# Four block normalisations of the first layer moved from VectorE to GpSimd in a four-layer attention and MLP kernel

## The chip, the cores and the metric

The kernel runs on one core of one Trainium2 chip. A core has TensorE (PE in the profile; PEld is its weight load), VectorE (DVE), ScalarE (ACT), GpSimd (POOL), SyncE (SP, which here only issues DMAs) and 16 DMA engines. The metric is the device time of one execution in microseconds; lower is better. Inputs and outputs lie in device memory (HBM).

## What is computed

A sequence of 2048 tokens with 448 features goes through four residual layers: attention A, gated MLP B, then A and B again with the same weights. Each layer starts with a layer norm without gain or bias. Attention is local and dilated: 16 heads of 28 features, and each query sees the 8 keys at distances 0, 2, ..., 14. The MLP multiplies two linear maps elementwise, without a nonlinearity.

```python
def _layernorm(x, axis=-1, eps=1e-5):
    m = jnp.mean(x, axis=axis, keepdims=True)
    v = jnp.var(x, axis=axis, keepdims=True)
    return (x - m) / jnp.sqrt(v + eps)
...
        pos = jnp.arange(S)
        off = jnp.arange(W) * dil
        idx = pos[:, None] - off[None, :]
        mask = idx >= 0
...
        logits = jnp.einsum("bhsd,bhswd->bhsw", q, kg) * scale
        logits = jnp.where(mask[None, None, :, :], logits, -1e9)
        attn = _softmax(logits, axis=-1)
        o = jnp.einsum("bhsw,bhswd->bhsd", attn, vg)
...
        g = jnp.einsum("bsd,df->bsf", x, w_gate)
        u = jnp.einsum("bsd,df->bsf", x, w_up)
        h = g * u
        return jnp.einsum("bsf,fd->bsd", h, w_down)
...
    x = A_x
    x = x + _A_ref(_layernorm(x, axis=-1), A_wqkv, A_wo)
    x = x + _B_ref(_layernorm(x, axis=-1), B_w_gate, B_w_up, B_w_down)
    x = x + _A_ref(_layernorm(x, axis=-1), A_wqkv, A_wo)
    x = x + _B_ref(_layernorm(x, axis=-1), B_w_gate, B_w_up, B_w_down)
    return x
```

## The kernel before

**Blocks and chunks.** The tokens are split by parity, so that a dilation of two becomes a plain neighbourhood: block B (0 to 15) is 128 tokens on 128 partitions, kept in `x_sb` in bf16. Layers are numbered 0 to 3 (attention 0 and 2, MLP 1 and 3). Each layer is cut into chunks of 256 or 512 tokens; in layer 0 chunk 0 is blocks 0 and 1, then 2 to 5, 6 to 9, 10 to 13, and 14 with 15.

**The norm of a block** (`ln_chunk`) has four steps. VectorE takes statistics (`bn_stats` at L630, `bn_aggr` at L632 into `mv`). ScalarE makes 1/sqrt(variance + eps) as a logarithm and an exponential (L633, L635, into `rstd`). One `tensor_scalar` (L651) subtracts the mean and multiplies by `rstd`, both per partition, and writes `xn_sb`, a ring of five slots; in layers 0 and 2 it is 512 elements wide, in layers 1 and 3 it is 896. Last, the block is transposed into `xnTa` or `xnTb`: by a DMA transpose from SyncE (L654), or, for the first four chunks of layer 0, by eight TensorE transposes (L661) whose result in PSUM ScalarE or VectorE copies out (L669).

**Attention of a chunk.** `qk_chunk` multiplies `xnTa` with the query-key weight `WQK` (L369, four units of 14 matmuls, each cut in two parts of 6 and 8) and copies the result to `qk` (L785). `WQK` is laid out in the kernel: L565 copies the staged weight (GpSimd, eight copies of 448 elements a partition; the same line's ScalarE form is two instructions, L566 and L567), and L575 fills the four unused columns of each head with a part of the value weight (eight small copies), which may only be done when TensorE has ended the first two chunks. `v_group` makes values (`v_sb`, L851, L856). The first three query blocks use small score matmuls (L915). The later ones use `attn_front2`: four key blocks (L970, or L969 on ScalarE) are made by multiplying `qk` by a 0/1 column `pm`, 256 or 512 elements wide, and TensorE multiplies them with the queries (L977); ScalarE takes exponentials (L922, L983), VectorE multiplies by a 0/1 band (L932 with `MK`, L992 with `MB`). `attn_back` multiplies with the values (L1010), adds the two halves and normalises (L1020, L1024, L1034 to L1055), and `y_blocks` projects and adds to `x_sb` (L1073). GpSimd builds the bands `MK` and `MB` at the start (selects L523 and sums L527, L547, L548).

**MLP of a chunk.** `b_chunk`: gate and up (L369 and L372 with `WGU`), a copy (L1109), the product (L1112), down (L369 with `WD`, or L1124 for the last two blocks), the addition (L1073, L1128).

**Order.** The program lists 1636 operations, each with the engines that may do it. What each engine does, and in which order, stands in a table of strings, `ORD`; a letter behind `!` picks which of several waits comes first, `+` and `@` mix the small matmuls of attention between those of the MLP. `BANK` gives the PSUM banks of each operation. Every engine runs its list in order and waits on semaphores, so an operation that is late holds all behind it on its engine. DMAs are issued by SyncE in the order of its list, apart from three by ScalarE.

Of the kernel before, what the change touches and what calls it, by code (L numbers as in the profile page):

```python
# [404 lines left out]
def build(nc, A_x, A_wqkv, A_wo, B_w_gate, B_w_up, B_w_down, out):  # L405
# [214 lines left out]
    def ln_chunk(li, j, prio):  # L620
# [17 lines left out]
        for B in blocks:  # L638
# [12 lines left out]
            sc.add("dve", one(lambda E, B=B, dst=dst, src=src: E.tensor_scalar(dst, src, mv[:, B, 0:1], rstd[:, B:B + 1], ALU.subtract, ALU.mult), ("xn", li, B)),  # L651
                   325.0 if par == 0 else 540.0, deps=[("rstd", li, B), ("mv", li, B), ("x", li - 1, B), prev], prio=prio - 0.2)
# [602 lines left out]
```

## Time and profile before

| | |
|---|---|
| runs | 380.07, 380.54, 381.71 us (median 380.54) |
| the profiled execution's own time | 379.54 us |
| its span, first to last instruction | 377.8 us |
| mean granted TensorE clock | 0.999 |
| TensorE before 10 us | busy 8.43 of 10.00 us (start-up, with warming matmuls) |
| GpSimd, longest idle stretches | 49.8, 37.0 and 35.8 us, all before L970 in the third layer |
| L651 on VectorE, 512 wide | 32 of them, 12.8 us |
| L970 on GpSimd, all shapes | 54 of them, 82.8 us |

The page's lines give the engine, source line, operation, `out<-in`, count, busy time and mean duration, and what ended the idle time before. VectorE is busy 73% over the whole span, but 9.75 of the ten microseconds from 10 to 20; the average hides that.

### The profile page before, as it was taken

The page shows a single profiled execution, that of the slowest core. Times are in us where ns is not written, and L with a number is a line of the kernel's source. Part 1 is how long each engine was busy: PE and PEld are TensorE (multiplying, and loading weights), DVE is VectorE, ACT ScalarE, POOL GpSimd, SP SyncE. Part 2 cuts the span into 40 slices and gives each one's busy share as a digit, 9 for nine tenths or more (in the row PEclk, how much of TensorE's full clock was granted, in tenths as well). Part 3 has the DMA queues.
Part 4 walks back from the last instruction along what each step waited for, and adds up shares of the span by engine and source line. Part 5 has one row for each costly group of instructions (what it writes and reads, how often), then busy time and mean ns, then how long its engine had stood idle before and what let it go on. Part 6 is the DMA issues. An engine that isn't in the chain of part 4 may idle for free.

```text
span 377.8 us, 13091 instructions
## 1 busy us (share of the span) xinstructions
PE 372.8 (99%) x5796; PEld 220.7 (58%) x5796; DVE 277.2 (73%) x571; ACT 203.9 (54%) x382; POOL 100.3 (27%) x123
## 2 busy tenths in 40 slices
PE   8999999999999999999999999999999999999997
PEld 4556587645556885545566577554455444455764
DVE  6999999797996874788876785758758884244433
ACT  3999996857328542464634554584686333124310
POOL 8735598710000610009300076003900000000000
PEclk9999999999999999999999999999999999999999
DMA  8883638201420162104142036200520025040002
GB/s 267 208 171 86 147 69 164 57 3 29 85 57 2 33 84 40 30 2 69 21 64 30 2 46 88 53 2 12 82 55 3 1 51 122 0 62 2 2 2 97
DMA packets 55099, 22.67 MB, mean 60 GB/s; under 512 B 46132, under 2 KB 54148, under 8 KB 55044
## 3 DMA queue, kind: packets, MB, share of 16 engines
q1 hardware_dynamic: 54612, 21.34, 28.7%
q8 instruction: 45, 0.74, 0.8%
q10 hardware_dynamic: 432, 0.52, 0.4%
q14 instruction: 10, 0.08, 0.1%
HBM read 8.54 MB, written 2.71 MB: 30 GB/s over the span
## 4 chain that ended last, share of the span: by engine, by line
PE 90%; DMA 3%; DVE 3%; SPq 2%; ACT 1%; POOL 0%; issue 0%
PE ps L369 83%; PE ps L1010 2%; PE ps L977 2%; PE ps L1124 1%; PE ps L372 1%; DMA x_sb<-in_A_x_dram 1%; DMA v_sb<-vt 1%; SPq L794 1%; SPq L805 1%; DVE st L630 1%; DMA vt<-qk 1%; ACT E_sb L983 1%; POOL WQK L575 0%; SPq L468 0%; DVE xn_sb L651 0%; PE ps L661 0%
## 5 line engine op out<-in xcount | busy, mean ns | idle before, releaser
L369 PE MATMUL ps<-xnTb,WGU 64*128 64x512 bf16 (+1 forms) x1928 | 177.4, 333 | 0.0
L369 PEld LDWEIGHTS ps<-xnTb,WGU 64*128 64x128 bf16 x1928 | 99.5, 94 | 63.4 <-ACT g_sb L1109 0.3
L1109 ACT ACTIVATE g_sb<-ps 128x512 bf16<-128x512 f32 (+1 forms) x140 | 69.2, 510 | 104.8 <-PE ps L369 96.0
L970 POOL TENSOR_SCALAR qk<-qk,pm 128x512 bf16<-128x512 bf16 (+1 forms) x51 | 77.9, 1544 | 159.2 <-DVE qk L785 64.5
L1112 DVE TENSOR_TENSOR hT<-g_sb,ps 128x512 bf16<-128x512 bf16 (+1 forms) x140 | 77.3, 573 | 54.6 <-ACT g_sb L1109 52.7
L369 PE MATMUL ps<-WD,hT 64*128 64x448 bf16 x828 | 85.9, 349 | 0.0
L369 PEld LDWEIGHTS ps<-WD,hT 64*128 64x128 bf16 x828 | 40.0, 94 | 34.5 <-ACT g_sb L1109 0.2
L369 PE MATMUL ps<-xnTa,WQK 64*128 64x512 bf16 (+1 forms) x504 | 54.0, 353 | 0.3 <-POOL WQK L565 0.2
L1073 DVE TENSOR_TENSOR x_sb<-x_sb,ps 128x448 bf16<-128x448 bf16 x62 | 36.5, 614 | 17.4 <-PE ps L369 17.0
L630 DVE BATCH_NORM_STATS2 st<-x_sb 128x6 f32<-128x448 bf16 x64 | 38.1, 614 | 2.1 <-DMA x_sb<-in_A_x_dram 1.8
L651 DVE TENSOR_SCALAR xn_sb<-x_sb,mv,rstd 128x896 bf16<-128x896 bf16 (+1 forms) x64 | 35.8, 574 | 3.8 <-ACT rstd L635 3.5
L983 ACT ACTIVATE E_sb<-ps 128x1024 bf16<-128x1024 f32 (+1 forms) x32 | 31.7, 996 | 9.6 <-PE ps L977 9.6
L369 PEld LDWEIGHTS ps<-xnTa,WQK 64*128 64x128 bf16 x504 | 25.1, 94 | 18.8 <-POOL WQK L565 0.4
L369 PE MATMUL ps<-wo_g,oT 64*128 64x448 bf16 x256 | 29.8, 349 | 0.0
L785 ACT ACTIVATE qk<-ps 128x1024 bf16<-128x1024 f32 (+1 forms) x27 | 25.0, 941 | 5.8 <-PE ps L369 5.7
L369 PE MATMUL ps<-WV,xnTa 64*128 64x336 bf16 (+3 forms) x252 | 22.8, 304 | 0.0
L1035 ACT ACTIVATE R_sb<-R_sb 128x960 f32<-128x960 f32 (+1 forms) x18 | 17.3, 959 | 8.1 <-DVE R_sb L1034 8.1
L992 DVE TENSOR_TENSOR E_sb<-E_sb,MB 128x1024 bf16<-128x1024 bf16 (+2 forms) x34 | 21.2, 634 | 0.4 <-ACT E_sb L983 0.3
L633 ACT ACTIVATE lnv<-mv,eps_sb 128x2 f32<-128x2 f32 (+1 forms) x33 | 9.4, 291 | 22.4 <-DVE mv L632 22.3
L1034 DVE STREAM_SHUFFLE R_sb<-O_sb 128x960 f32<-128x960 f32 (+1 forms) x18 | 21.1, 1181 | 0.0
L1055 DVE TENSOR_TENSOR oT<-O_sb,R_sb 128x960 bf16<-128x960 f32 (+1 forms) x16 | 17.6, 1104 | 4.5 <-ACT R_sb L1036 4.5
L369 PEld LDWEIGHTS ps<-wo_g,oT 64*128 64x128 bf16 x256 | 13.5, 94 | 10.1 <-issue 0.2
(67 smaller groups left out, 239.4 us busy)
## 6 DMA issues: line engine op xcount, KB each, us to landing
out_dram<-x_sb SPq DMA_DIRECT2D x15, 112.0 KB, 1.8
WGU<-in_B_w_gate_dram SPq DMA_DIRECT2D x7, 224.0 KB, 4.3
WGU<-in_B_w_up_dram SPq DMA_DIRECT2D x7, 224.0 KB, 3.8
x_sb<-in_A_x_dram SPq DMA_DIRECT2D x3, 448.0 KB, 6.3
WD<-in_B_w_down_dram SPq DMA_DIRECT2D x2, 448.0 KB, 3.9
vt<-qk SPq DMA_DIRECT2D x42, 16.0 KB
WD<-in_B_w_down_dram SPq DMA_DIRECT2D x2, 336.0 KB, 4.2
xnTb<-xn_sb SPq DMA_TRANSPOSE x32, 3.1
```

The lines of the kernel that those rows point to most:

```text
L369: return lambda E: E.matmul(out(), lhs(), rhs(), start=start, stop=stop)
L630: sc.add("dve", one(lambda E, B=B: E.bn_stats(st6[:, B, :], x_sb[:, B, :]), ("bn", li, B)), 525.0, deps=[("x", li - 1, B)] + ([("xn", li - ...
L651: sc.add("dve", one(lambda E, B=B, dst=dst, src=src: E.tensor_scalar(dst, src, mv[:, B, 0:1], rstd[:, B:B + 1], ALU.subtract, ALU.mult), ( ...
L785: return E.activation(dst, src, ACT.Copy) if hasattr(E, "activation") else E.tensor_copy(dst, src)
L970: return E.tensor_scalar(dst, src, pm[:, t:t + 1], None, ALU.mult)
L983: return E.activation(E_sb[:, slot, 2 * c:2 * c + 2, 0:w], ps[:, bk[0]:bk[0] + 2, 0:w], ACT.Exp, scale=SCALE)
L992: return E.tensor_tensor(e, e, m, ALU.mult)
L1034: sc.add("dve", one(lambda E: E.stream_shuffle(R_sb[:, rs, 0:w], O_sb[:, op, 0:w], [DH] * 32), ("Rs", li, g)), dve_est(w) + 100.0, deps=[( ...
L1055: return E.tensor_tensor(oT[:, :, t:t + n].rearrange("p h (d n) -> p h d n", d=nd), O, R, ALU.mult)
L1073: sc.add("dve", one(lambda E: E.tensor_tensor(x_sb[:, B, :], x_sb[:, B, :], ps[:, bk[w], 0:D], ALU.add), ("x", li, B)), dve_est(D), deps=[ ...
L1109: sc.add("act", one(lambda E, gs=gs, bk=bk: E.activation(g_sb[:, gs, 0:nt], ps[:, bk[0], 0:nt], ACT.Copy), ("G", li, j, fc)), act_est(nt), ...
L1112: sc.add("dve", one(lambda E, gs=gs, bk=bk, fc=fc: E.tensor_tensor(hT[:, fc, hs, 0:nt], g_sb[:, gs, 0:nt], ps[:, bk[1], 0:nt], ALU.mult), ...
```

## The change

In `ln_chunk`, the L651 norm of layer 0 may now be done by GpSimd for blocks 4 to 15. The table then gives it blocks 8, 9, 11 and 14. All of `ORD` and `BANK` is replaced: every engine's list has the same operations for the most part, with neighbours exchanged all through the program. TensorE's matmuls are the same in number and shape. Besides the four norms, these change engines: in layer 0, the copies of three transposed blocks (7, 9, 11) go from ScalarE to VectorE, one L565 copy from GpSimd to ScalarE, two L575 copies from GpSimd to VectorE, two key blocks from VectorE to GpSimd and two the other way; in layer 2, 26 key blocks leave GpSimd (15 to VectorE, 11 to ScalarE), and 3 go from ScalarE to VectorE. Of the copies out of PSUM, 12 go from ScalarE to VectorE and 15 the other way. GpSimd's list shrinks from 119 instructions to 92.

**GpSimd between its masks and its first key blocks.** `MK`, `MB` and `hT` with L523 are mask work, `WQK` is the small weight copies, L970 the key blocks. Before:

```order
L547 TENSOR_TENSOR MB<-hT 128x72 [waits sem_pool]
L523 AFFINE_SELECT hT<-hT 128x72
L527 TENSOR_TENSOR MK<-hT 128x72 [waits sem_pool]
L575 COPY WQK<-hT 128x16x4 [waits sem_pe,sem_d_stv]
L575 COPY WQK<-hT 128x16x4 x3
L575 COPY WQK<-hT 128x4x3x4 x4
L970 TENSOR_SCALAR hT<-qk,pm 128x4x2x64 [waits sem_dve]
```

Now:

```order
L547 TENSOR_TENSOR MB<-hT 128x72 [waits sem_pool]
L651 TENSOR_SCALAR xn_sb<-x_sb,mv,rstd 128x512 [waits sem_act]
L547 TENSOR_TENSOR MB<-hT 128x72
L523 AFFINE_SELECT hT<-hT 128x72
L651 TENSOR_SCALAR xn_sb<-x_sb,mv,rstd 128x512
L651 TENSOR_SCALAR xn_sb<-x_sb,mv,rstd 128x512 [waits sem_pe,sem_act]
L575 COPY WQK<-hT 128x4x3x4 [waits sem_pe,sem_d_stv]
L575 COPY WQK<-hT 128x4x3x4 x2
L548 AFFINE_SELECT MB<-MB 128x72
L575 COPY WQK<-hT 128x16x4
L575 COPY WQK<-hT 128x4x3x4
L523 AFFINE_SELECT hT<-hT 128x72
```

and right behind it:

```order
L575 COPY WQK<-hT 128x16x4
L527 TENSOR_TENSOR MK<-hT 128x72
L651 TENSOR_SCALAR xn_sb<-x_sb,mv,rstd 128x512 [waits sem_pe]
L523 AFFINE_SELECT hT<-hT 128x72
L970 TENSOR_SCALAR hT<-qk,pm 128x4x2x64 [waits sem_act]
```

The norms of blocks 9, 8 and 14 now stand ahead of the small weight copies, that of block 11 behind them; two of the eight copies are gone to VectorE, and two selects stand among the six that are left.

**TensorE around the first steps that need the whole of `WQK`.** L661 transposes a block, L915 are scores, L1010 is the product with the values. Before:

```order
L661 MATMUL ps<-hT,xn_sb 128x64 [waits sem_act]
L661 MATMUL ps<-hT,xn_sb 128x64 x7
L1010 MATMUL ps<-E_sb,v_sb 32x72 [waits sem_dve]
L1010 MATMUL ps<-E_sb,v_sb 32x72 x31
L915 MATMUL ps<-qk 64x64 [waits sem_act,sem_dve]
L915 MATMUL ps<-qk 64x64 x63
L369 MATMUL ps<-xnTa,WQK 128x512 [waits sem_act,sem_pool]
L369 MATMUL ps<-xnTa,WQK 128x512 x5
L369 MATMUL ps<-xnTa,WQK 128x512 [waits sem_dve]
L369 MATMUL ps<-xnTa,WQK 128x512 x5
L661 MATMUL ps<-hT,xn_sb 128x64 [waits sem_act]
```

Now:

```order
L1010 MATMUL ps<-E_sb,v_sb 32x72 x31
L661 MATMUL ps<-hT,xn_sb 128x64 [waits sem_dve]
L661 MATMUL ps<-hT,xn_sb 128x64 x7
L915 MATMUL ps<-qk 64x64 [waits sem_act,sem_dve]
L915 MATMUL ps<-qk 64x64 x63
L369 MATMUL ps<-xnTa,WQK 128x512 [waits sem_dve,sem_pool]
L369 MATMUL ps<-xnTa,WQK 128x512 x5
L369 MATMUL ps<-xnTa,WQK 128x512 [waits sem_dve]
L369 MATMUL ps<-xnTa,WQK 128x512 x5
L369 MATMUL ps<-xnTa,WQK 128x512 [waits sem_pe]
L369 MATMUL ps<-xnTa,WQK 128x512 x7
L661 MATMUL ps<-hT,xn_sb 128x64 [waits sem_pool,sem_act]
```

The transpose of block 7 moved from ahead of the product with the values (L1010) to behind it, directly ahead of the scores. The last row is block 11's transpose: it now waits for GpSimd, and one more part of eight matmuls stands ahead of it.

**GpSimd's key blocks of the third layer**, L970 towards the end of its list. Before:

```order
L970 TENSOR_SCALAR qk<-qk,pm 128x4x64 [waits sem_act]
L970 TENSOR_SCALAR qk<-qk,pm 128x4x64
L970 TENSOR_SCALAR qk<-qk,pm 128x4x2x64 x3
L970 TENSOR_SCALAR qk<-qk,pm 128x4x64
L970 TENSOR_SCALAR qk<-qk,pm 128x4x2x64 [waits sem_act,sem_dve]
L970 TENSOR_SCALAR qk<-qk,pm 128x4x2x64 x2
L970 TENSOR_SCALAR qk<-qk,pm 128x4x2x64 [waits sem_pe]
L970 TENSOR_SCALAR qk<-qk,pm 128x4x2x64 x4
```

Now:

```order
L970 TENSOR_SCALAR qk<-qk,pm 128x4x2x64 [waits sem_pe]
L970 TENSOR_SCALAR qk<-qk,pm 128x4x2x64
L970 TENSOR_SCALAR qk<-qk,pm 128x4x2x64 [waits sem_dve,sem_act]
L970 TENSOR_SCALAR qk<-qk,pm 128x4x2x64 [waits sem_act]
L970 TENSOR_SCALAR qk<-qk,pm 128x4x2x64
L1204 UNCONDITIONAL_BRANCH
```

Three key blocks are left on GpSimd in that layer, of 29; the first piece shows the first 14 of them, the second the last two key blocks of the first layer and the three that are left.

The diff, with the tables cut to GpSimd's list:

```diff
 ORD = {
...
-    "pool": "18 43 20 19 23 24 25 26 27 28 29 90 91 94 95 92 96 93 97 49 53 50 22 67 60 34 38 51 35 31 64 54 39 65 40 68 21 32 66 30 69 61 62 57 55 41 58 59 33 70 63 52 56 36 37 100 102 98 104 105 103 101 99 299 71 42 300 409 426 431 432 427 553 554 581 559 558 576 628 634 633 580 575 651 650 629 656 655 801 796 820 819 814 797 961 967 989 1175 984 983 988 1174 1202 1201 1354 1179 1197 1353 1180 1196 1381 1375 1380 1376 1398 1402 1403",
+    "pool": "18 43 20 19 23 24 25 26 27 28 29 90 91 94 95 92 96 93 30 21 31 34 49 50 53 60 35 67 57 32 38 58 54 64 22 61 51 62 68 39 55 65 69 33 52 59 63 190 56 36 187 223 103 101 105 71 104 99 66 98 37 208 40 299 41 70 295 294 427 409 426 42 431 432 554 576 581 559 558 633 628 580 634 575 629 651 650 655 656 819 1197 1196",
...
 }
...
@@ -648,8 +648,8 @@
                 c0 = 512 * (nbs[(li, j)] % 2) + 128 * B - t0
                 war = xslot_users.get(nbs[(li, j)] % 2, [])
             nt = 4 if par == 0 else 7
-            sc.add("dve", one(lambda E, B=B, dst=dst, src=src: E.tensor_scalar(dst, src, mv[:, B, 0:1], rstd[:, B:B + 1], ALU.subtract, ALU.mult), ("xn", li, B)),
-                   325.0 if par == 0 else 540.0, deps=[("rstd", li, B), ("mv", li, B), ("x", li - 1, B), prev], prio=prio - 0.2)
+            sc.add(("dve", "pool") if li == 0 and B > 3 else "dve", one(lambda E, B=B, dst=dst, src=src: E.tensor_scalar(dst, src, mv[:, B, 0:1], rstd[:, B:B + 1], ALU.subtract, ALU.mult), ("xn", li, B)),
+                   {"dve": 325.0, "pool": 1620.0} if li == 0 and B > 3 else 325.0 if par == 0 else 540.0, deps=[("rstd", li, B), ("mv", li, B), ("x", li - 1, B), prev], prio=prio - 0.2)
             if not by_pe:
```

More of the change, by code (lines that the diff above doesn't have):

```diff
@@ L60 @@
 ORD = {
[5 rows of a table removed]
[5 rows of a table added]
 }
-BANK = "72:1 138:23 142:45 158:67 161:67 164:67 167:45 182:23 185:45 188:01 191:01 206:01 209:01 212:01 215:01 227:67 229:01 231:23 233:45 239:01 243:4501 248:23 256:45 258:67 260:67 262:23 268:23 272:01 277:0167 282:45 290:23 296:67 301:45 304:23 312:45 326:62 329:01 332:23 335:67 338:41 341:01 344:06 347:57 350:50 353:74 356:21 359:67 362:34 365:10 368:54 374:67 376:45 378:23 380:23 393:67 398:23 406:01 411:67 414:01 422:23 428:23 433:01 436:23 444:23 468:72 471:67 474:34 477:54 480:17 483:10 486:46 489:05 492:14 495:50 498:76 501:71 504:64 507:50 510:75 516:23 522:67 524:45 526:01 528:45 541:67 547:01 555:45 560:23 563:45 571:65 577:67 582:23 585:23 593:10 597:01 599:67 601:45 603:23 616:67 622:23 630:23 635:01 638:45 646:23 652:23 657:45 660:67 668:67 692:01 695:51 698:40 701:45 704:36 707:01 710:72 713:60 716:23 719:07 722:14 725:56 728:27 731:14 734:32 740:20 766:45 768:01 770:67 772:01 785:45 790:23 798:23 803:23 806:01 816:67 821:45 824:67 832:72 856:16 859:45 862:45 865:13 868:01 871:63 874:60 877:45 880:27 883:24 886:17 889:17 892:60 895:60 898:27 904:07 930:67 932:23 934:45 936:01 949:23 955:45 963:01 968:01 971:45 979:26 985:23 990:23 993:45 1001:10 1015:41 1018:31 1021:60 1024:23 1027:64 1030:64 1033:36 1036:51 1039:23 1042:45 1045:10 1048:01 1051:01 1054:06 1057:03 1073:67 1076:72 1079:23 1082:67 1085:14 1088:56 1091:25 1094:14 1097:03 1100:54 1103:21 1106:52 1109:43 1112:10 1115:45 1143:67 1145:45 1147:23 1149:23 1162:67 1168:45 1176:45 1181:67 1184:01 1192:67 1198:67 1203:67 1206:67 1214:01 1238:03 1241:56 1244:45 1247:72 1250:76 1253:13 1256:14 1259:10 1262:23 1265:67 1268:05 1271:52 1274:35 1277:42 1280:46 1288:01 1316:67 1318:23 1320:45 1322:45 1335:01 1341:23 1347:45 1355:67 1360:67 1363:67 1371:64 1377:01 1382:67 1385:67 1393:15 1399:23 1404:23 1407:01 1415:27 1439:52 1442:45 1445:03 1448:37 1451:46 1454:40 1457:57 1460:34 1463:16 1466:52 1469:52 1472:63 1475:17 1478:04 1481:01 1489:63 1517:45 1520:27 1523:54 1526:27 1529:63 1532:57 1535:54 1538:24 1541:45 1544:63 1547:47 1550:27 1553:47 1556:52 1559:71 1567:23 1585:61 1588:10 1591:71 1594:63 1597:50 1600:10 1603:10 1606:50 1609:54 1612:61 1615:24 1618:02 1621:53 1624:46 1627:6 1630:7 1633:0"
@@ new lines @@
+BANK = "72:2 138:01 142:45 158:45 161:23 164:23 167:01 182:45 185:67 188:45 191:45 206:67 209:01 212:01 215:67 227:01 229:67 231:23 233:01 239:67 243:2367 248:23 256:23 258:01 260:01 262:67 268:45 272:67 277:4501 282:01 290:23 296:45 301:01 304:45 312:01 326:24 329:67 332:45 335:23 338:17 341:67 344:62 347:30 350:36 353:01 356:03 359:52 362:54 365:32 368:54 374:45 376:67 378:23 380:23 393:45 398:45 406:67 411:23 414:67 422:74 428:45 433:67 436:01 444:67 468:01 471:01 474:75 477:45 480:23 483:42 486:15 489:40 492:40 495:67 498:35 501:14 504:05 507:67 510:61 516:05 522:23 524:01 526:67 528:01 541:23 547:23 555:01 560:45 563:01 571:46 577:67 582:01 585:67 593:74 597:45 599:67 601:01 603:23 616:67 622:23 630:67 635:23 638:67 646:67 652:23 657:01 660:23 668:45 692:14 695:34 698:12 701:76 704:12 707:23 710:50 713:72 716:04 719:45 722:71 725:07 728:06 731:15 734:63 740:76 766:23 768:45 770:67 772:01 785:23 790:01 798:23 803:01 806:45 816:01 821:01 824:01 832:56 856:53 859:24 862:45 865:23 868:01 871:70 874:23 877:41 880:65 883:67 886:54 889:12 892:60 895:30 898:24 904:04 930:45 932:23 934:45 936:01 949:67 955:23 963:23 968:23 971:67 979:31 985:45 990:23 993:01 1001:54 1015:67 1018:61 1021:53 1024:25 1027:63 1030:17 1033:53 1036:23 1039:65 1042:45 1045:20 1048:70 1051:45 1054:35 1057:10 1073:61 1076:04 1079:42 1082:23 1085:42 1088:26 1091:75 1094:34 1097:31 1100:34 1103:25 1106:02 1109:41 1112:53 1115:54 1143:23 1145:67 1147:23 1149:67 1162:67 1168:01 1176:67 1181:67 1184:23 1192:01 1198:67 1203:67 1206:67 1214:23 1238:21 1241:56 1244:45 1247:70 1250:10 1253:21 1256:04 1259:32 1262:13 1265:67 1268:34 1271:50 1274:14 1277:50 1280:04 1288:23 1316:01 1318:23 1320:45 1322:45 1335:67 1341:67 1347:45 1355:67 1360:67 1363:67 1371:40 1377:23 1382:67 1385:45 1393:23 1399:67 1404:01 1407:23 1415:56 1439:15 1442:01 1445:61 1448:67 1451:70 1454:41 1457:37 1460:26 1463:05 1466:70 1469:25 1472:43 1475:67 1478:14 1481:30 1489:12 1517:46 1520:47 1523:67 1526:65 1529:71 1532:07 1535:56 1538:53 1541:67 1544:04 1547:50 1550:25 1553:56 1556:32 1559:64 1567:70 1585:13 1588:04 1591:54 1594:41 1597:24 1600:32 1603:35 1606:63 1609:64 1612:15 1615:10 1618:23 1621:75 1624:21 1627:1 1630:0 1633:7"
```

8 rows, old and new, of the table ORD are left out of this document.

## The prediction

> **What bounds the kernel now.** The page comes first: its busy shares, and its chain that ended last.
>
> ```profile
> PE 372.8 (99%) x5796; PEld 220.7 (58%) x5796; DVE 277.2 (73%) x571; ACT 203.9 (54%) x382; POOL 100.3 (27%) x123
> PE 90%; DMA 3%; DVE 3%; SPq 2%; ACT 1%; POOL 0%; issue 0%
> ```
>
> TensorE is busy 372.8 of 377.8 us and holds 90% of the chain; GpSimd (POOL) holds none of it. Where TensorE has any room is told by the view of busy time by stretches (stretch, length, busy us of PE, PEld, DVE, ACT, POOL, then granted clock and DMA).
>
> ```profile
> 9.00:16.00 7.00, 6.92 (x142) 4.13 (x138) 6.75 (x23) 6.43 (x19) 6.78 (x33) 1.00 1.07 272
> 16.00:20.00 4.00, 4.00 (x55) 1.93 (x52) 4.00 (x13) 3.77 (x11) 0.72 (x3) 1.00 0.40 107
> 20.00:23.00 3.00, 2.50 (x130) 1.63 (x128) 2.99 (x10) 2.98 (x6) 1.70 (x8) 1.00 0.86 200
> 23.00:100.00 77.00, 76.82 (x1462) 47.68 (x1458) 70.93 (x146) 61.41 (x105) 37.73 (x25) 1.00 0.41 85
> 100.00:280.00 180.00, 180.00 (x2792) 109.72 (x2790) 135.67 (x274) 93.92 (x177) 45.44 (x31) 1.00 0.26 42
> ```
>
> From 9 to 280 us TensorE idles 0.08 + 0.50 + 0.18 = 0.76 us, most of it between 20 and 23, where VectorE (2.99 of 3.00) and ScalarE (2.98) are full. So hardly anything can be won after the start-up, and the question is what the change makes TensorE wait for. TensorE's timeline shows when it wants the blocks that move:
>
> ```profile
> 16.70 0.28 PE L661 MATMUL ps<-hT,xn_sb 64*128 64x64 bf16 x8
> 16.82 2.54 PE L369 MATMUL ps<-xnTa,WQK 64*128 64x512 bf16 x22
> 19.19 0.28 PE L661 MATMUL ps<-hT,xn_sb 64*128 64x64 bf16 x8
> 19.31 1.03 PE L369 MATMUL ps<-xnTa,WQK 64*128 64x512 bf16 x8
> 20.17 0.62 PE L661 MATMUL ps<-hT,xn_sb 64*128 64x64 bf16 x24
> 22.42 1.47 PE L369 MATMUL ps<-xnTa,WQK 64*128 64x512 bf16 x12
> 23.73 0.28 PE L661 MATMUL ps<-hT,xn_sb 64*128 64x64 bf16 x8
> ...
> 28.02 3.88 PE L369 MATMUL ps<-xnTa,WQK 64*128 64x256 bf16 x62
> ```
>
> L661 transposes a normalised block, eight matmuls each: block 9 at 16.70, block 8 at 19.19, block 11 at 23.73. The L369 at 22.42 is the first query-key step that needs all of the weight WQK, including the pieces that GpSimd copies (L575). Block 14 goes by a DMA transpose and is wanted only by the step at 28.02.
>
> **The change part by part.** GpSimd's own rows, before:
>
> ```profile
> 3.98 4.31 POOL L565 COPY WQK<-hT 128x448 bf16<-128x448 bf16 x8
> 8.23 0.46 POOL L508 MEMSET hT<- 128x432 bf16 x1
> 16.48 0.32 POOL L527 TENSOR_TENSOR MK<-hT 128x72 bf16<-128x72 bf16 x1
> 20.51 0.24 POOL L575 COPY WQK<-hT 128x64 bf16<-128x64 bf16 x1 [3.70 <-PE ps L661]
> 20.90 1.46 POOL L575 COPY WQK<-hT 128x64 bf16<-128x64 bf16 x7 [0.16 <-issue]
> ```
>
> GpSimd ends its masks at 16.80, idles 3.70 us until TensorE releases the weight pieces at 20.51, and ends those at 22.36, just before the step at 22.42. Into that gap go the norms. What a norm costs on GpSimd no row shows. The nearest are its key blocks (L970: same width and types, one multiplication by a per-partition scalar; the norm has a subtraction and a multiplication, with two scalars). The second row below is GpSimd between 48 and 65 us, without a gap and beside a full VectorE:
>
> ```profile
> L970 POOL TENSOR_SCALAR hT<-qk,pm x3: 1558/1570/1679, 26.5 to 34.5; 128x512 bf16<-128x512 bf16 x3
> L970 POOL TENSOR_SCALAR qk<-qk,pm 128x512 bf16<-128x512 bf16 x11 | 17.8, 1632 | 4.6 <-PE ps L977 4.6
> L970 POOL TENSOR_SCALAR qk<-qk,pm 128x256 bf16<-128x256 bf16 x7 | 6.7, 963 | 49.8 <-ACT qk L785 49.8
> L565 POOL COPY WQK<-hT 128x448 bf16<-128x448 bf16 x8 | 4.3, 574 | 0.1
> L523 POOL TENSOR_SCALAR_AFFINE_SELECT hT<-hT 128x72 bf16<-128x72 bf16 x34 | 7.6, 256 | 0.5
> L547 POOL TENSOR_TENSOR MB<-hT 128x72 bf16<-128x72 bf16 x3 | 0.9, 318 | 0.1
> L651 DVE TENSOR_SCALAR xn_sb<-x_sb,mv,rstd 128x512 bf16<-128x512 bf16 x32 | 12.8, 417 | 0.9 <-ACT rstd L635 0.6
> L970 DVE TENSOR_SCALAR hT<-qk,pm 128x512 bf16<-128x512 bf16 x3 | 1.2, 408 | 0.0
> ```
>
> Lower end: a norm costs what a key block costs, 1.57 us alone, 1.63 loaded. Upper end: the second operation doubles the work per element. From 963 to 1632 ns over 256 elements is 2.61 ns per element and 0.29 us fixed, so 0.29 + 512 x 5.22 ns = 2.96 us. Between them: a copy with the same fixed part takes (574 - 290) / 448 = 0.63 ns per element, so one operation adds 1.98; a second one adding as much gives 0.29 + 512 x 4.59 ns = 2.64 us. I take 1.63, because it is the same engine, operation and shape, and because on VectorE the two forms cost nearly the same (417 and 408 ns). That is a choice, and the range keeps both ends.
>
> The Trainium skill (GPSIMD Engine Reference, 3.1) gives 512 elements 769 ns at best and holds bodies of up to two operations to the same port limit. This trace's 1570 ns for one operation is twice that; by the skill's page a second operation is free, and the sum would be the one below.
>
> Now the queue. One weight copy goes to ScalarE: GpSimd's seven end at 3.98 + 4.31 x 7/8 = 7.75. Of the 8.57 us from 8.23 to 16.80, three mask sums (318) and four selects (256), 1.98 us, move behind the first norm. So norm 9 starts at 7.75 + 8.57 - 1.98 = 14.34 and ends at 15.97, 0.73 before it is wanted. Its scale factor is there by then:
>
> ```profile
> 14.07 0.19 ACT L635 ACTIVATE rstd<-lnv 128x2 f32<-128x2 f32 x1
> ```
>
> A sum and a select later (0.57), norm 8 runs from 16.54 to 18.17, 1.0 early; norm 14 ends at 19.80. The weight pieces wait for TensorE until 20.51 anyway: 0.71 us of cover for three norms, 0.24 each. Behind them stand six pieces and two selects instead of eight pieces:
>
> ```profile
> L575 POOL COPY WQK<-hT 128x48 bf16<-128x48 bf16 x4 | 0.9, 274 | 0.0
> L575 POOL COPY WQK<-hT 128x64 bf16<-128x64 bf16 x4 | 0.8, 236 | 3.9 <-PE ps L661 3.7 <-issue 0.2
> ```
>
> 4 x 0.274 + 2 x 0.236 + 2 x 0.256 = 2.08 against 4 x 0.274 + 4 x 0.236 = 2.04: the step at 22.42 comes some 0.1 later. Then one mask sum, and norm 11 from 22.75 to 24.38. The changed order puts one eight-matmul step (19.31 to 20.17, 0.86 us) ahead of block 11's transpose, which is thus wanted at 23.73 + 0.1 + 0.86 = 24.69: 0.3 of cover. With d the price of a norm above 1.63, TensorE loses 0.1 + max(0, 3d - 0.71) + max(0, d - 0.3) us.
>
> VectorE loses four norms (4 x 0.417 = 1.67 us) and gains three transposed copies from ScalarE and two weight pieces:
>
> ```profile
> L669 DVE COPY xnTa<-ps 128x512 bf16<-128x512 bf16 x7 | 2.8, 418 | 0.3 <-PE ps L661 0.2
> L669 ACT ACTIVATE xnTa<-ps 128x512 bf16<-128x512 bf16 x5 | 3.0, 596 | 0.5 <-PE ps L661 0.5
> ```
>
> 3 x 0.418 is 1.25; with two pieces of at most 0.24 that is 1.7, so VectorE keeps its load and ScalarE sheds 3 x 0.596. The waits of 20 to 23 could shrink, by 0.5 at most, or grow by as much, as block 7's transpose and its copy now stand right ahead of the scores (L915). I take nothing.
>
> In the third layer 26 key-block copies leave GpSimd for VectorE (15) and ScalarE (11), and three more go from ScalarE to VectorE. On VectorE one takes 0.61 (below), so 18 x 0.61 = 11.0 us in a stretch of 180 where it has 44.3 idle; ScalarE's net 8 x 0.72 = 5.8 stands against 86.1 idle. I take nothing; if a copy came late at a step, each slip would cost about one copy, 0.6 to 0.7.
>
> ```profile
> L970 DVE TENSOR_SCALAR qk<-qk,pm 128x512 bf16<-128x512 bf16 x3 | 1.8, 610 | 0.0
> L969 ACT ACTIVATE qk<-qk,pm 128x512 bf16<-128x512 bf16 x3 | 2.1, 714 | 0.8 <-DVE qk L785 0.8
> 375.54 0.35 ACTq L468 DMA_DIRECT2D out_dram<-x_sb x1
> ```
>
> SyncE issues the last outputs in another order, but the end is ScalarE's store at 375.54, behind the last matmul: nothing. The sum: span 377.8 + 0.1 = 377.9, with 1.74 around it (379.54 - 377.8) 379.6 for such an execution. The median of the runs is 1.0 above the profiled one, so 380.6; I say 380.8, since of the open terms more can lose than win.
>
> **The rivals.** *The norm's second operation is dear* (the other side). Place: GpSimd's queue ahead of the weight pieces. At 2.64 us d is 1.01: 0.1 + 2.32 + 0.71 = 3.1 us, 383.7; at 2.96, 0.1 + 3.28 + 1.03 = 4.4, 385.0. It decides from 1.87 on and passes 0.5% at 2.33 (4 x 0.70 - 1.01 + 0.1 = 1.9). For it: copy to one operation multiplies GpSimd's cost per element by four. Against: VectorE's two rows.
>
> *VectorE is held by a norm.* Its mask products (L932, two inputs from SBUF) now run beside norm 8. If each waited for the norm's end, up to 1.63 us, with VectorE full, TensorE would lose about 1.5: 382.3. Against it: L992, the same product, takes 672 ns beside a busy GpSimd and 678 without.
>
> ```profile
> L992 DVE TENSOR_TENSOR E_sb<-E_sb,MB 128x1024 bf16<-128x1024 bf16 x3 | 2.0, 672 | 0.0
> L992 DVE TENSOR_TENSOR E_sb<-E_sb,MB 128x1024 bf16<-128x1024 bf16 x5 | 3.3, 678 | 0.0
> ```
>
> The Trainium skill (SBUF — State Buffer, Who interferes with whom) says that the second to issue fully blocks. By it this rival holds; these rows disagree.
>
> *A late key block in the third layer*: two slips, +1.4, 382.1.
>
> *VectorE's relief counts*: the 0.5 of 20 to 23 goes, 380.1. With TensorE full elsewhere, no more is there.
>
> **How the numbers follow.** Chances: forecast 0.44, dear norm 0.40, held VectorE 0.05, late key blocks 0.06, relief 0.05. What a measurement can tell from no change is about 0.5%, 1.9 us. The dear norm is over that in nine of ten of its part (0.36), the two others in most (0.07), the forecast in a little (0.01): slower 0.44. Faster would need more idle time than TensorE has: 0.03. Within 0.5%: 0.53. The forecast's own range is 380.0 to 381.8; with the dear norm most of the way it is 379.9 to 384.6.
>
> **What would show it.** In the changed profile: L651 on GpSimd, four times; at 1.6 us the weight pieces still start at 20.5 after a wait for TensorE, and the full query-key step at 22.5. At 2.3 or more GpSimd reaches them late without a wait, and TensorE's stretch of 20 to 26 us shows idle time put down to GpSimd's L575 or L651. L932 well over 0.44 would speak for the held VectorE. The forecast is wrong if TensorE idles over 2 us more than before anywhere after 9 us, or if the time falls by more than 1.

## The result, and the profile after

| | changed | before, same comparison | ratio (95% interval) |
|---|---|---|---|
| first comparison | 380.87 us | 380.06 us | 1.0025 (1.0015 to 1.0035) |
| second comparison | 380.66 us | 379.95 us | 1.0020 (1.0010 to 1.0030) |

The change costs 0.7 to 0.95 us of 380: slower by a hair, within the half per cent that was called no change. Three of its 22 executions in the first comparison were disturbed (392, 786 and 998 us), the profiled one among them, so the ratio leaves them out and every row of the changed kernel below is from the second. The profiled execution there took 380.49 us; its span is 378.8 us, 1.0 more than that of before.

First the page of the changed kernel: busy shares, and the shares of the chain that ended last.

```profile
PE 373.0 (98%) x5796; PEld 216.7 (57%) x5796; DVE 283.6 (75%) x591; ACT 207.5 (55%) x390; POOL 67.4 (18%) x96
PE 86%; DVE 6%; POOL 3%; issue 2%; DMA 1%; SPq 0%
```

GpSimd's busy time falls by a third, and yet it now holds 3% of the chain, where it held none. Next the busy time by stretches, the same stretches and columns as in the prediction.

```profile
9.00:16.00 7.00, 6.97 (x144) 4.17 (x140) 6.61 (x23) 6.11 (x19) 6.81 (x26) 1.00 0.92 241
16.00:20.00 4.00, 4.00 (x56) 2.00 (x52) 3.92 (x15) 3.84 (x10) 4.00 (x5) 1.00 0.62 156
20.00:23.00 3.00, 2.37 (x128) 1.45 (x126) 3.00 (x12) 2.59 (x5) 3.00 (x11) 1.00 0.40 83
23.00:100.00 77.00, 76.30 (x1446) 46.68 (x1444) 71.22 (x142) 61.00 (x105) 40.82 (x28) 1.00 0.45 91
100.00:280.00 180.00, 180.00 (x2782) 106.07 (x2778) 138.05 (x289) 99.31 (x186) 4.88 (x3) 1.00 0.25 41
```

TensorE's idle time from 9 to 280 us is 0.03 + 0.63 + 0.70 = 1.36 us instead of 0.76. Between 16 and 23 GpSimd is now full (4.00 and 3.00). But the larger growth, from 0.18 to 0.70, lies after 23 us, where no norm is left but one.

Where the delay arises is read from the starts of matmuls that both programs run in the same order. TensorE's timeline before, later than the rows that the prediction shows:

```profile
47.73 0.93 PE L369 MATMUL ps<-wo_g,oT 64*128 64x448 bf16 x8
51.63 0.41 PE L977 MATMUL ps<-qk 64*128 64x64 bf16 x16
64.84 2.82 PE L369 MATMUL ps<-WD,hT 64*128 64x448 bf16 x28
```

And of the changed kernel:

```profile
22.76 2.33 PE L369 MATMUL ps<-xnTa,WQK 64*128 64x512 bf16 x20 [0.47 <-POOL WQK L575]
25.19 0.29 PE L661 MATMUL ps<-hT,xn_sb 64*128 64x64 bf16 x8
48.39 0.93 PE L369 MATMUL ps<-wo_g,oT 64*128 64x448 bf16 x8
52.74 0.41 PE L977 MATMUL ps<-qk 64*128 64x64 bf16 x16 [0.33 <-DVE x_sb L1073]
56.82 0.40 PE L977 MATMUL ps<-qk 64*128 64x64 bf16 x16
66.24 1.50 PE L369 MATMUL ps<-WD,hT 64*128 64x448 bf16 x14
```

The delay is 0.34 us at the full query-key step (22.42), 0.66 at the first projection (47.73), 1.11 at the query-key scores of 51.63 and 1.40 at 64.8. By the end 0.4 of it has come back in small pieces. So there are two clear places: the GpSimd queue that the prediction worked on, and one at 48 to 53 us that it did not. The last step, from 1.11 to 1.40, is a third that stays unclear: at 60.95 us the delay is down to 0.86 (the same L1010 had waited 0.18 us for a DMA before, at 60.09), and of the growth behind it the profile shows only a stop of TensorE of 0.19 us at 63.49, for which it gives no cause. GpSimd's own timeline shows the first:

```profile
14.50 2.08 POOL L651 TENSOR_SCALAR xn_sb<-x_sb,mv,rstd 128x512 bf16<-128x512 bf16 x1
21.20 0.54 POOL L575 COPY WQK<-hT 128x48 bf16<-128x48 bf16 x3
22.47 0.23 POOL L575 COPY WQK<-hT 128x64 bf16<-128x64 bf16 x1
22.97 2.07 POOL L651 TENSOR_SCALAR xn_sb<-x_sb,mv,rstd 128x512 bf16<-128x512 bf16 x1
```

The weight pieces start at 21.20, without a wait for TensorE, 0.69 later than before (20.51), and TensorE waits 0.47 us for them at 22.76. The next rows are the groups of GpSimd by line and shape: the norm takes 2.09 us, not 1.63.

```profile
L651 POOL TENSOR_SCALAR xn_sb<-x_sb,mv,rstd 128x512 bf16<-128x512 bf16 x4 | 8.4, 2093 | 0.0
L575 POOL COPY WQK<-hT 128x48 bf16<-128x48 bf16 x4 | 0.8, 219 | 0.0
```

### The profile page after: what moved, and what is told of

Its sections match the earlier page's. It is cut to its first block, busy times and chain, and to the rows that moved or that the text cites. A ratio compares the mean times of both kernels' runs of the same rounds, so it can differ in the third digit from the quotient of the medians.

```text
span 996.5 us, 13084 instructions
## 1 busy us (share of the span) xinstructions
PE 992.5 (100%) x5796; PEld 407.4 (41%) x5796; DVE 290.1 (29%) x591; ACT 213.6 (21%) x390; POOL 65.1 (7%) x96
## 4 chain that ended last, share of the span: by engine, by line
PE 99%; DVE 0%; issue 0%; DVEq 0%
PE ps L369 93%; PE ps L977 2%; PE ps L1124 1%; PE ps L372 1%; PE ps L1010 1%; PE ps L555 1%; PE ps L661 0%; DVE xnTa L669 0%; DVE WQK L575 0%; DVE x_sb L1128 0%; DVE xn_sb L651 0%; DVE hT L508 0%; PE ps L915 0%; DVE eps_sb L508 0%; DVEq L342 0%
## 5 line engine op out<-in xcount | busy, mean ns | idle before, releaser
L369 PE MATMUL ps<-xnTb,WGU 64*128 64x512 bf16 (+1 forms) x1924 | 470.1, 708 | 0.0
L369 PEld LDWEIGHTS ps<-xnTb,WGU 64*128 64x128 bf16 x1924 | 180.6, 169 | 259.0 <-issue 216.6
L369 PE MATMUL ps<-WD,hT 64*128 64x448 bf16 x832 | 227.5, 754 | 0.0
L369 PE MATMUL ps<-xnTa,WQK 64*128 64x512 bf16 (+1 forms) x504 | 141.7, 762 | 0.2 <-DVE WQK L575 0.2
L369 PEld LDWEIGHTS ps<-WD,hT 64*128 64x128 bf16 x832 | 75.1, 169 | 129.4 <-issue 125.7
L1073 DVE TENSOR_TENSOR x_sb<-x_sb,ps 128x448 bf16<-128x448 bf16 x62 | 36.7, 617 | 179.5 <-PE ps L369 179.5
L369 PE MATMUL ps<-wo_g,oT 64*128 64x448 bf16 x256 | 75.3, 758 | 0.0
L970 POOL TENSOR_SCALAR qk<-qk,pm 128x512 bf16<-128x512 bf16 x22 | 34.4, 1580 | 484.4 <-ACT qk L785 422.6
L369 PE MATMUL ps<-WV,xnTa 64*128 64x336 bf16 (+3 forms) x252 | 56.8, 626 | 0.0
L651 DVE TENSOR_SCALAR xn_sb<-x_sb,mv,rstd 128x896 bf16<-128x896 bf16 (+1 forms) x60 | 35.0, 597 | 9.1 <-ACT rstd L635 8.9
L977 PEld LDWEIGHTS ps<-qk 64*128 64x128 bf16 x432 | 23.3, 149 | 15.8 <-issue 14.3
L977 PE MATMUL ps<-qk 64*128 64x64 bf16 (+1 forms) x432 | 23.9, 285 | 0.0
```

Source lines behind the costliest of these rows:

```text
L369: return lambda E: E.matmul(out(), lhs(), rhs(), start=start, stop=stop)
L651: sc.add(("dve", "pool") if li == 0 and B > 3 else "dve", one(lambda E, B=B, dst=dst, src=src: E.tensor_scalar(dst, src, mv[:, B, 0:1], rs ...
L970: return E.tensor_scalar(dst, src, pm[:, t:t + 1], None, ALU.mult)
L977: ins.append((lambda E, hc=hc, d=d, p=p, c=c, qs=qs, o=o, bk=bk: E.matmul(ps[:, bk[p], o:o + nc], KB[64 * p:64 * p + 64, hc, d, c, :], qk[ ...
L1073: sc.add("dve", one(lambda E: E.tensor_tensor(x_sb[:, B, :], x_sb[:, B, :], ps[:, bk[w], 0:D], ALU.add), ("x", li, B)), dve_est(D), deps=[ ...
```

## Experiments

Two theories stood against each other. *H*: the whole loss is the norms on GpSimd, ahead of 31 us. *K*: the larger part is one key block that has gone from GpSimd to VectorE at 48 us, where VectorE has no room. In `ORD`, 190, 187, 223 and 208 are the norms of blocks 9, 8, 14 and 11; 553 is that key block. The expectations call it the second layer's, since it runs beside layer 1's first chunks; it belongs to the last attention chunks of layer 0.

### The changed kernel again

No edit; its rows are those above.

> The changed kernel again, for an undisturbed profile. Theory 1 (dear norm in GpSimd's queue): a norm on GpSimd took 2.08 us in the disturbed profile, 0.45 above the 1.63 that the prediction took, so TensorE loses 0.1 + (3 x 0.45 - 0.71) + (0.45 - 0.30) = 0.9 us between 20 and 26 us: GpSimd reaches its small weight copies at about 21.1 without a wait for TensorE, the full query-key step starts at about 23.2 instead of 22.4, and behind it TensorE is about 1 us later than before in all that follows. Theory 2 (the rest of the reordering): TensorE is level with before at 27 us and loses 0.9 us later, most of it in the third layer, where 26 key blocks left GpSimd. Either way the time is 1.0025 of before.

380.66 us, ratio 1.0020 (1.0010 to 1.0030).

### One operation instead of two

```diff
-one(lambda E, ...: E.tensor_scalar(dst, src, mv[:, B, 0:1], rstd[:, B:B + 1], ALU.subtract, ALU.mult), ...)
+one(lambda E, ...: E.tensor_scalar(dst, src, mv[:, B, 0:1], None, ALU.subtract) if li == 0 and B in (8, 9, 11, 14) else
+                   E.tensor_scalar(dst, src, mv[:, B, 0:1], rstd[:, B:B + 1], ALU.subtract, ALU.mult), ...)
```

> The norms of blocks 8, 9, 11 and 14 on GpSimd only subtract the mean and leave out the multiplication by the scale factor; the order is that of the changed kernel. Theory 1: a norm on GpSimd takes 1.57 us like a key block, GpSimd is in time for the weight copies again, and the time is 0.1 to 0.3 us above before (ratio 1.0003 to 1.0008). Theory 2: nothing that matters is taken away, ratio 1.0025 as for the changed kernel.

This kernel leaves out the multiplication by `rstd`. 380.32 us, 0.34 below the changed kernel in the same comparison, ratio to before 1.0015 (1.0003 to 1.0027). GpSimd's group, then TensorE's timeline:

```profile
L651 POOL TENSOR_SCALAR xn_sb<-x_sb,mv 128x512 bf16<-128x512 bf16 x4 | 6.5, 1631 | 0.3 <-ACT rstd L635 0.2
```

```profile
28.22 0.68 PE L1010 MATMUL ps<-E_sb,v_sb 64*32 64x64 bf16 x64 [0.23 <-DVE xnTa L669]
```

With one operation the norm costs exactly the 1.63 us of a key block: the second operation is 2.09 - 1.63 = 0.46 us. The time does not decide between the theories: its interval overlaps that of the changed kernel, and also the 1.0003 to 1.0008 that was expected if the norm's price were all. In the trace the wait for the weight pieces is gone, but one for VectorE's copy has appeared at 28.2 us. The first projection starts at 48.26 us, only 0.13 ahead of the changed kernel's; 0.28 us of that execution's delay was there already at 14.47 us (L915, 14.19 in the changed kernel), before its first norm on GpSimd began.

### The norm of block 14 twice

```diff
-sc.add(..., one(lambda E, ...: E.tensor_scalar(dst, ...), ("xn", li, B)), ...)
+sc.add(..., [(lambda E, ..., dst=(xd_sb if n < k - 1 else dst): E.tensor_scalar(dst, ...), ("xn", li, B) if n == k - 1 else None)
+             for k in [2 if li == 0 and B == 14 else 1] for n in range(k)], ...)
```

> GpSimd does the norm of block 14 twice, the first time into a buffer that nobody reads: 2.08 us more ahead of the small weight copies. Theory 1: the cover is used up already, so all of the 2.08 comes out at the end: 380.06 + 0.9 + 2.1 = 383.0 us, ratio 1.008, and the full query-key step starts at about 25.2. Theory 2: the wait there is hidden or made good later, ratio near 1.0025.

384.06 us, ratio 1.0111 (1.0087 to 1.0135): 3.4 us above the changed kernel for 2.15 us more work on GpSimd. TensorE's timeline:

```profile
24.88 4.02 PE L369 MATMUL ps<-xnTa,WQK 64*128 64x512 bf16 x20 [2.47 <-POOL WQK L576]
```

The queue is what the step waits for: it starts 24.88 - 22.76 = 2.12 later, one norm. The rest is the granted clock: after 2.47 us of waiting, the same 20 matmuls that took 2.33 us take 4.02, and the transpose behind them is 3.54 us later (28.73 against 25.19). The expected 383.0 us had the queue alone (the clock itself is shown in the last section).

### The norm of block 14 back on VectorE

```diff
-"dve": "... 225 186 102 199 251 ..."    "pool": "... 190 56 36 187 223 103 ..."
+"dve": "... 225 186 102 223 199 251 ..." "pool": "... 190 56 36 187 103 ..."
```

> The norm of block 14 goes back to VectorE, behind its part of the small weight copies; GpSimd keeps those of 9, 8 and 11. Theory 1: GpSimd has two norms ahead of the weight copies, is done at 19.1 and waits for TensorE until 20.5; what is left is 0.1 for the copies and 0.15 for block 11, so 380.3 us, ratio 1.0007, plus up to 0.4 if VectorE, full there, hands on the 0.42 us of the norm. Theory 2: ratio 1.0025 or more, since VectorE has more to do.

381.40 us, ratio 1.0039 (1.0017 to 1.0061), a miss. Six of twelve executions took 380.03 to 380.66 us, near what was expected, six 382.15 to 384.27. The profiled one (382.86) is of the second kind (TensorE's timeline, and one stretch of the busy times; the granted clock stands behind the five engines):

```profile
23.37 0.32 PE L915 MATMUL ps<-qk 28*64 28x64 bf16 x28 [0.89 <-issue]
23.62 4.02 PE L369 MATMUL ps<-xnTa,WQK 64*128 64x512 bf16 x20
```

```profile
23.00:26.00 3.00, 2.63 (x40) 1.09 (x41) 1.92 (x7) 2.13 (x4) 3.00 (x4) 0.63 0.43 87
```

GpSimd is in time there (it waits 1.69 us for TensorE before its weight pieces), as expected. But TensorE stops for 0.89 us inside its scores for nothing that the profile shows, and then runs 20 matmuls at half clock. Why it stops there is open, and whether the other five long executions are the same was not seen.

### Half of each order

The tables of the two kernels were joined at one time of the trace of before: all operations that start earlier there come in one kernel's order, all others in the other's.

```diff
 ORD, BANK   changed after 31 us:   start below 31 us: before;  all others: changed
 ORD, BANK   changed before 31 us:  start below 31 us: changed; all others: before
 ORD, BANK   changed after 75 us:   start below 75 us: before;  all others: changed
```

> Every engine's order and the PSUM banks are those of the kernel before up to about 31 us of its trace (all norms on VectorE), and those of the changed kernel afterwards. Theory H (the loss of about 0.8 us is the norms in GpSimd's queue and arises before 31 us): as before, ratio 1.000, within 0.0006. Theory K (it arises between 45 and 66 us, where one key block of the second layer has gone from GpSimd to a full VectorE): ratio 1.002, some 380.7 us. Reading of the changed profile (TensorE's lag behind its own work grows by 0.6 us before 31 us, by 0.7 to 0.8 between 45 and 66, and falls by 0.3 between 190 and 280): +0.5 us, ratio 1.0012, and in its profile TensorE's idle time of 45 to 66 us as in the changed kernel, that of 16 to 31 us as before.

> The counterpart: the changed kernel's order up to about 31 us (four norms on GpSimd), that of the kernel before afterwards. Theory H: the whole loss, ratio 1.0022, some 380.8 us. Theory K: as before, ratio 1.000, within 0.0006. Reading of the changed profile: +0.6 us, ratio 1.0016, the full query-key step again about 0.35 us late behind GpSimd's weight pieces, and VectorE's second-layer rows as before.

> The order of the kernel before up to about 75 us, that of the changed kernel afterwards: only the third layer's moves are left (its key blocks off GpSimd). Theories H and K both: no loss, ratio 1.000. Reading of the changed profile: a gain of 0.3 us, ratio 0.9993, which would make it the fastest of all; a loss of 0.3 or more would mean that the third layer's copies do cost something.

381.44 us, ratio 1.0038 (1.0024 to 1.0053); 380.69, 1.0030 (1.0011 to 1.0048); 381.58, 1.0040 (1.0025 to 1.0056). The first and the third are not what either theory said, and their profiles say why: the join makes waits of its own. TensorE's waits in the first (rows of its timeline) and in the third (its list of waits: total, times, longest):

```profile
33.16 0.41 PE L977 MATMUL ps<-qk,hT 64*128 64x64 bf16 x16 [1.09 <-DVE qk L785]
53.50 0.41 PE L977 MATMUL ps<-qk 64*128 64x64 bf16 x16 [0.33 <-DVE x_sb L1073]
```

```profile
PE ps L369 <- ACT v_sb L856: 1.8, 1, 1.8
```

1.09 us at 33.16 and 1.8 us stand in neither whole kernel, so these two times decide nothing. What can be read is the rows away from the join. With the changed order only after 31 us, the wait of 0.33 us before L977 is there as in the changed kernel. With it only before 31 us, that wait is absent, and of the head's the one at the weight pieces is left. That run's interval (0.4 to 1.8 us) holds the 0.6 read from the changed profile and excludes the no loss that K alone expects, but it can't size the head: in its profile TensorE is 0.44 us late at the first projection (48.17), and a stop without a cause then adds to it:

```profile
22.58 0.61 PE L369 MATMUL ps<-xnTa,WQK 64*128 64x512 bf16 x4 [0.23 <-POOL WQK L575]
63.52 1.47 PE L369 MATMUL ps<-xnTb,WGU 64*128 64x256 bf16 x23 [0.93 <-issue]
```

So the two places don't need each other.

### One key block alone

```diff
 before.py
-"dve": "... 416 417 311 418 400 ..."      "pool": "... 432 427 553 554 581 559 558 576 ..."
+"dve": "... 416 417 311 553 418 400 ..."  "pool": "... 432 427 554 581 559 558 576 ..."
```

> The kernel before with one instruction moved: the first key block of the second layer's queue, on GpSimd at 47.37 us, goes to VectorE between the output product (L1055, 46.43) and the shuffle (L1034, 47.52), where the changed kernel has it. Theory K: it takes 0.35 to 0.8 us of a VectorE that is busy 28.68 of 29.00 us there, all behind it comes as much later, and TensorE waits for the residual sums (L1073) before L977 at about 52 us: +0.4 to +0.8 us, ratio 1.001 to 1.002. Theory H: no loss, ratio 1.000, since GpSimd's relief by 1.6 us and VectorE's extra 0.4 have room elsewhere.

380.82 against 380.12 us, ratio 1.0015 (1.0003 to 1.0027): +0.7 us for one instruction, with 0.1 to 1.0 by the interval; the profiled execution's span is 0.7 longer too (378.5). VectorE's timeline before, then with the block moved (its last row is TensorE's):

```profile
47.52 1.23 DVE L1034 STREAM_SHUFFLE R_sb<-O_sb 128x960 f32<-128x960 f32 x1
50.34 1.15 DVE L1073 TENSOR_TENSOR x_sb<-x_sb,ps 128x448 bf16<-128x448 bf16 x2
```

```profile
47.44 0.78 DVE L970 TENSOR_SCALAR qk<-qk,pm 128x512 bf16<-128x512 bf16 x1
48.14 1.26 DVE L1034 STREAM_SHUFFLE R_sb<-O_sb 128x960 f32<-128x960 f32 x1
50.99 1.15 DVE L1073 TENSOR_TENSOR x_sb<-x_sb,ps 128x448 bf16<-128x448 bf16 x2
52.29 0.41 PE L977 MATMUL ps<-qk 64*128 64x64 bf16 x16 [0.34 <-DVE x_sb L1073]
```

The block takes 0.78 us, so the residual sums (L1073) come 0.65 later, and TensorE, which waited for nothing at 51.63, waits 0.34 and starts at 52.29. All norms are on VectorE in this run, so H alone falls. There is no room to absorb the block, as the stretch of 31 to 60 us before shows (VectorE 28.68 of 29.00):

```profile
31.00:60.00 29.00, 28.91 (x590) 19.06 (x584) 28.68 (x57) 26.22 (x44) 20.87 (x13) 1.00 0.48 116
```

### The key block given back, and what is left then

```diff
 changed kernel
-"dve": "... 417 311 553 418 401 ..."  "pool": "... 431 432 554 576 581 559 558 ..."
+"dve": "... 417 311 418 401 ..."      "pool": "... 431 432 553 554 576 581 559 558 ..."
 and, in the second run, the one operation of above; in the third, instead:
-"dve": "... 225 186 102 199 251 ..."          "pool": "... 187 223 103 ... 37 208 40 299 ..."
+"dve": "... 225 186 102 223 208 199 251 ..."  "pool": "... 187 103 ... 37 40 299 ..."
```

> The changed kernel with the one second-layer key block given back from VectorE to the head of GpSimd's queue of that stage. Theory K (that block is the larger part of the loss): TensorE's wait of 0.33 us before L977 at 52.7 us is gone, 0.6 to 0.7 us faster than the changed kernel, ratio to before 1.0005 (some 380.3 us). Theory H (the loss is the norms on GpSimd): nothing is won, ratio 1.002.

> The same, and the four norms on GpSimd only subtract the mean; the multiplication by rstd is left out. If the head's loss is the price of the norm's second operation: another 0.3 to 0.6 us faster, ratio 0.9995 to 1.000. If the head's loss is the order around it (with one operation TensorE had waited for VectorE's copy at 28.2 us instead): the same time as with two operations, within 0.2 us.

> The key block back on GpSimd, and norms 14 and 11 back on VectorE behind its weight pieces: only 8 and 9 stay on GpSimd. By the sum (loss 0.1 + max(0, 3d - 0.71) + max(0, d - 0.3), with d = 0.45 and now without norms 14 and 11) nothing but the 0.1 is left: ratio 1.0003. If VectorE, full from 20 to 23 us, decides instead: its two norms (0.8 us) push the scores (L915) and the second-layer copies back, ratio 1.001 to 1.003, with single executions 2 us longer where TensorE's idle time there lowers the granted clock to 0.5.

381.01 us, ratio 1.0028 (1.0013 to 1.0044); 381.16, 1.0037 (1.0020 to 1.0054); 381.54, 1.0038 (1.0024 to 1.0052). Giving the block back wins nothing, against what K expected. TensorE and GpSimd in the first of the three:

```profile
47.94 9.63 POOL L970 TENSOR_SCALAR qk<-qk,pm 128x512 bf16<-128x512 bf16 x6 [4.45 <-PE ps L977]
48.38 0.93 PE L369 MATMUL ps<-wo_g,oT 64*128 64x448 bf16 x8
52.18 0.41 PE L977 MATMUL ps<-qk 64*128 64x64 bf16 x16
57.71 0.41 PE L977 MATMUL ps<-qk 64*128 64x64 bf16 x16 [1.30 <-DVE oT L1055]
```

The wait at 52.2 is gone, as expected, but the next L977 waits 1.30 us. The row puts it down to VectorE's L1055, but GpSimd's six blocks end at 47.94 + 9.63 = 57.57, 0.14 ahead of the step at 57.71. The changed kernel tells the two apart: there GpSimd's first five end, in its timeline, at 47.99 + 7.89 = 55.88, and the same step starts at 56.82, before L1055 even begins (VectorE's row).

```profile
47.99 7.89 POOL L970 TENSOR_SCALAR qk<-qk,pm 128x512 bf16<-128x512 bf16 x5 [4.45 <-PE ps L977]
56.89 1.15 DVE L1055 TENSOR_TENSOR oT<-O_sb,R_sb 128x960 bf16<-128x960 f32 x1
```

So the step doesn't need L1055, and what is left in its way is GpSimd's sixth block. The tables fit that: before, block 576 stands behind 559 and 558, and five blocks are due by that step; the change has pulled 576 ahead of them, which made a sixth, and 553 had to go elsewhere. On this reading the block on VectorE is the price of a reordering. Giving both back (553 to GpSimd, 576 behind 558), which would test it, was not tried.

One operation against two, with the block back, shows the head by itself: the first projection starts at 47.95 instead of 48.38 us.

```profile
22.30 2.33 PE L369 MATMUL ps<-xnTa,WQK 64*128 64x512 bf16 x20
24.46 0.29 PE L661 MATMUL ps<-hT,xn_sb 64*128 64x64 bf16 x8
47.95 0.93 PE L369 MATMUL ps<-wo_g,oT 64*128 64x448 bf16 x8
```

Of the 0.66 us that the head loses in the changed kernel, 0.43 are the second operation of the norm, and 0.22 (47.95 - 47.73) the order around it. The pair without the block back (48.39 and 48.26) agrees if the early 0.28 us are taken off: 0.13 + 0.28 = 0.41. The times of the runs don't resolve this pair. Two norms put back on VectorE give a median 0.5 us higher still, with overlapping intervals. In that profile GpSimd is in time (it waits 1.96 us for TensorE), and yet the first projection starts at 49.15, 0.77 later than with only the block back. TensorE's waits for VectorE's copy (0.19) and ScalarE's (0.24) are no longer than before (0.18 and 0.27), while two stops without a cause, of 0.22 and 0.33 us, are new. So whether VectorE has a place for these norms is open.

### Only the third layer's moves

```diff
 ORD, BANK   start below 120 us: before; all others: changed
```

> The order of the kernel before up to about 120 us, that of the changed kernel afterwards, so that the seam lies where VectorE and ScalarE have room. If the third layer's key blocks are free or a small gain: ratio 0.9993 to 1.000 (379.8 to 380.1 us), and TensorE's lag from 130 us to the end smaller than before by 0.2 us. If they cost: a stall of 0.6 us or more in the stretch behind the seam.

380.66 us, ratio 1.0012 (0.9996 to 1.0029): inconclusive. The join costs a wait here too (the second row), and a DMA is late once:

```profile
PE ps L1010 <- DMA v_sb<-vt: 0.5, 1, 0.5
PE ps L369 <- DVE qk L785: 0.4, 1, 0.4
```

No version was faster than the kernel before.

## Why the prediction was right, and where it was not

**The time.** Said 380.8 us, measured 380.87, and the range holds it. Part of that is luck: the sum was +0.1 on a median of 380.54, and beside the changed kernel before took 380.06. The loss that was forecast is 0.1 to 0.3 us, the measured one 0.7 to 0.95.

**The norm's price** is the term that was mis-sized. The prediction chose 1.63 us; it is 2.09, between that and the 2.64 of the dear norm, above the 1.87 from which that rival was to decide and below the 2.33 at which it passes half a per cent. By the prediction's own mark it is thus the dear norm that came, in a mild form: GpSimd reaches the weight pieces late and without a wait, and the time stayed within half a per cent because the price was small. The choice by analogy with VectorE (417 against 408 ns for two and one operations) was wrong for GpSimd: the second operation costs 0.46 us there, by the experiment with one operation (1.63). The Trainium skill (GPSIMD Engine Reference, 3.1), by which up to two operations meet the same limit, doesn't hold here.

**The queue formula held.** With d = 2.09 - 1.63 = 0.46 it says that the weight pieces start 3 x 0.46 - 0.71 = 0.67 late; they did by 0.69. The step behind them was only 0.34 late, since the pieces were quicker than priced: six of them and two selects from 21.20 to 22.70, 1.50 us instead of 2.08 (the narrow ones 219 ns each, not 274). Norm 11 was wanted as soon as it was ready (22.97 + 2.07 = 25.04; the transpose at 25.19): from the full step to that transpose it takes 2.43 us, with one operation 2.16, so 0.27 late, where the formula has 0.16. The sum would have been 0.1 + 0.67 + 0.16 = 0.93 us for the head, against 0.66 measured.

**What was left out** is a second loss: 1.11 - 0.66 = 0.45 us in the changed kernel. The prediction priced the key blocks that VectorE takes over against 44.3 us of idle time in the third layer, and that part was right: they took less than the 0.61 that was assumed (a median of 346 ns, last section), and from 100 to 280 us TensorE idles nowhere. But one more stands at 48 us, in layer 0, where VectorE is full. The text on the change had counted the two key blocks of layer 0 that go to VectorE; the sum never placed them. It is the prediction's late key block, which it had put at 0.6 to 0.7 for each slip, but in another layer. Alone it costs 0.7 us. That this is the second place is shown (the block moved by itself, +0.66 at L977); that giving it back alone would cure the changed kernel is refuted.

**VectorE held by a norm** did not come. The two mask products that run beside a norm (from 17.66 us, norm 8 from 17.05) are the narrow ones; they take 450 ns, where they took 438 before (first row), and the sign for this rival was a time well over 0.44 us.

```profile
L932 DVE TENSOR_TENSOR E_sb<-E_sb,MK 128x576 bf16<-128x576 bf16 x2 | 0.9, 438 | 0.0
L932 DVE TENSOR_TENSOR E_sb<-E_sb,MK 128x576 bf16<-128x576 bf16 x2 | 0.8, 450 | 0.0
```

**Relief of VectorE** bought nothing: from 20 to 23 us it is as full as before (3.00 of 3.00), with the copies and weight pieces that came in the norms' place.

**Open:** how the last 0.4 us come back after 65 us, the growth of the delay between 60 and 65 us, and the unexplained stops of TensorE.

## What to carry to other kernels

Price an operation on another engine by a row of that engine with the same number of operations; if there is none, the bounds decide the chances, not an analogy with a third engine. When a change replaces an order, place each moved instruction in its own stretch: one 0.8 us instruction in a full stretch cost, by itself, as much as four norms in a queue with cover. And look at why an odd move was made before undoing it alone, since it may pay for a neighbour.
